# Stacks of k and q made while PSUM is emptied, f32 scores for four pairs, and the lower gate on GpSimd, in a new order of work

## The chip, the cores and the metric

One kernel runs on one core of a Trainium2 chip. The core has TensorE (PE; its weight loads are shown apart as PEld), VectorE (DVE), ScalarE (ACT), GpSimd (POOL) and SyncE (SP), each with its own queue of instructions that it takes in order; the engines wait for each other through semaphores. All DMAs of this kernel are issued by SyncE. The metric is the time of one execution on the device in microseconds, from first to last; lower is better.

## The reference

Attention over 4 batches of 8 heads, sequence 1152, head size 64, in which two neighbouring queries are averaged, followed by a two-layer network with a gate:

```
q_pool = q.reshape(B, H, S // 2, 2, D).mean(axis=3)        # 576 queries per head
scores = scale * q_pool @ k.T                              # 576 x 1152 per head
attn   = exp(scores - max); attn = attn / (sum + 1e-9)
x      = (attn @ v) as 2304 tokens of 512
h      = x @ w_in                                          # 512 -> 2048
g      = h * clip(h + 3, 0, 6) / 6
out    = g @ w_out                                         # 2048 -> 512
```

All inputs and the output are f32.

## The kernel before

**Attention.** Two heads of one batch make a pair; there are 16 pairs g. A pair has two halves h of 288 queries, and a half has two heads j; a unit u = (g, h, j) is one head's 288 queries against its 1152 keys, in 9 tiles t of 128 keys. Scores lie with keys on the partitions and queries in the columns. TensorE multiplies at f32r, one pass over 288 columns. To keep f32's precision, k and q are split into an upper part rounded to f32r (`kh`, `qh`) and the rest (`kl`, `ql`). The 128 partitions of a product hold 64 dimensions of the upper k and under them the same 64 of the lower k; q's upper part stands there twice, so that a first product takes both parts of k times `qh`, and a second one takes them times `ql` (L377).

The way to these stacks: `turn_k` (L324) and `turn_q` (L348) transpose a pair's k and pooled q on TensorE into PSUM, with one head in partitions 0 to 63 and the other in 64 to 127. `split` copies the upper part out on ScalarE (L330) and subtracts it on VectorE (L333). Since the halves have to go to other partitions, `move_k` (L340) and `move_q` (L355) then copy them from SBUF to SBUF by DMA: 12 DMAs per pair for k, 16 for q.

A unit goes on: `keep` copies a score tile from PSUM to SBUF on ScalarE (`copy`, L303), `most` takes the running maximum over tiles on VectorE (L390; for the first 15 units two key tiles at a time, with one fold at L394), `fold`, `best` and `spread` (L400, L404, L410) turn it into one maximum per query and lay it over all partitions, `lessen` (L414, VectorE) subtracts it, `expo` (L418, ScalarE) takes the exponential, `total` (L428, GpSimd) adds up over the tiles in four adds, `values` (L435) multiplies by v in f32, the two heads in two column groups of the array. `sums` (L452), `recip`, `widen`, `quotient` (L471) and `divide` (L475) scale the result; `split_x` and `spill` store it as f32r upper and lower part. `sums` frees the two tiles that the adds of the next half take.

**Network.** w_in and w_out are split once into upper and lower part by bit operations (`convert`: ScalarE, GpSimd, VectorE, L512 to L536), stored to DRAM (`save_w`) and loaded again for every 256 columns of x. A layer step m is one block of 128 hidden units for 256 tokens: `layer` (L184, 12 products), `relu` (L189, ScalarE), `gate` (L193, VectorE), `upper` (L197, ScalarE), `lower` (L202, the gated value minus its upper part; VectorE or GpSimd), and later `project` (L217, 6 products). 96 such steps are planned beside attention; the last 768 tokens follow in a loop of their own, with `lower` on VectorE.

**Order.** Nearly the whole program is a list of steps with a place (priority), costs per engine, needs, rooms taken and rooms freed. `Order.run` simulates the engines with these costs and so writes down one order for each engine; a tile framework adds the semaphores. `lower` may go to VectorE or GpSimd; its place there is 9 later (`NGL`). PSUM is divided anew once, at the step `second`: before it, attention has wide score tiles; after it, three banks for scores and banks for the network.

Of the kernel before, what the change touches and what calls it, by code (L numbers as in the profile page):

```python
# [11 lines left out]
F32 = mybir.dt.float32  # L12
F32R = mybir.dt.float32r
# [24 lines left out]
class Order:  # L38
# [14 lines left out]
    def run(self):  # L53
# [20 lines left out]
        while len(out) < len(steps):  # L74
# [4 lines left out]
            for e in engines:  # L79
# [20 lines left out]
                for b in frees:  # L100
                    if isinstance(b, tuple):
                        halves[b] = max(halves.get(b, 0), t + end + self.WAKE)
                        half[b] = half.get(b, 0) + 1
                        if half[b] < 2:
                            continue
# [22 lines left out]
def pooled_attention_then_gated_mlp(ctx, tc, q, k, v, w_in, w_out, out):  # L128
# [128 lines left out]
    with ExitStack() as a:  # L257
# [68 lines left out]
        def split(eng, tag, key, shape):  # L326
            ps = tr_t[key]
            if eng == "ACT":
                st = tr_t["st", key] = [ld.tile(shape, F32R, tag=tag + x, name=tag + x, bufs=2 if tag == "k" else 1) for x in "hl"]
                nc.scalar.copy(out=st[0], in_=ps)  # L330
            else:
                h, low = tr_t["st", key]
                nc.vector.tensor_tensor(out=low, in0=tr_t.pop(key), in1=h.bitcast(F32), op=ALU.subtract)  # L333

        def move_k(eng, g, c):
            if c == 0:
                kT[g] = kq.tile([P, 2, KT, P], F32R, tag="kT", name="kT")
            for n, x in enumerate(tr_t.pop(("st", ("k", g, c)))):
                for j in range(2):
                    nc.sync.dma_start(  # L340
                        out=kT[g][n * D:(n + 1) * D, j, KC * c:KC * (c + 1), :].bitcast(F32), in_=x[j * D:(j + 1) * D].bitcast(F32)
                    )

        def turn_q(eng, g, h):
            ps = tr_t["q", g, h] = space(g, HQ)
            for t in range(TQ):
                src = qp_t[g][:, h * TQ + t, :, :].rearrange("p j d -> p (j d)")
                nc.tensor.transpose(ps[:, t * QP:(t + 1) * QP], src, ident[:QP, :QP])  # L348

        def move_q(eng, g, h):  # L350
            q_t[g, h] = [qq.tile([P, 2, HQ], F32R, tag=t, name=t) for t in ("qh", "ql")]
            for x, to in zip(tr_t.pop(("st", ("q", g, h))), q_t[g, h]):
                for n in range(2):
                    for j in range(2):
                        nc.sync.dma_start(  # L355
                            out=to[n * D:(n + 1) * D, j, :].bitcast(F32), in_=x[j * D:(j + 1) * D].bitcast(F32)
                        )

        def index(u):
            return 4 * u[0] + 2 * u[1] + u[2]  # L360
# [18 lines left out]
        def keep(eng, u, t, end):  # L379
            if t == 0:  # L380
# [427 lines left out]
```

## Time and profile before

| | |
|---|---|
| median of 3 runs | 1052.11 us (1051.94 to 1064.61) |
| the profiled execution | 1051.82 us, its span 1050.0 us |
| mean granted TensorE clock | 0.927 |
| PE busy | 914.0 us (87%) |
| DVE busy | 709.1 us (68%) |
| ACT busy | 572.5 us (55%) |
| POOL busy | 500.2 us (48%) |
| DMA moved | 241.80 MB |
| chain of waits | PE 51%, DMA 22%, DVE 10%, issue 7%, ACT 5%, SPq 3% |

The span is the time from the first to the last instruction. "Busy" joins overlapping instructions of one engine; matmuls are pipelined and their ends are modelled. The chain of waits is followed back from the last instruction, at each step to what released it. In rows of busy time by stretch the engines stand as PE, PEld, DVE, ACT, POOL, each with its busy time and the count of its instructions. The granted clock is 1.00 where TensorE's clock is at its upper level. The pairs' first score products start at 20.5 us (pair 0), 61.3, 107.7, 151.2 and 202.7 us (pair 4); the first layer step at 235.5 us, and the last loop at 918.8 us.

### The profile page before, as it was taken

The page shows a single profiled execution, that of the slowest core. Times are in us where ns is not written, and L with a number is a line of the kernel's source. Part 1 is how long each engine was busy: PE and PEld are TensorE (multiplying, and loading weights), DVE is VectorE, ACT ScalarE, POOL GpSimd, SP SyncE. Part 2 cuts the span into 40 slices and gives each one's busy share as a digit, 9 for nine tenths or more (in the row PEclk, how much of TensorE's full clock was granted, in tenths as well). Part 3 has the DMA queues.
Part 4 walks back from the last instruction along what each step waited for, and adds up shares of the span by engine and source line. Part 5 has one row for each costly group of instructions (what it writes and reads, how often), then busy time and mean ns, then how long its engine had stood idle before and what let it go on. Part 6 is the DMA issues. An engine that isn't in the chain of part 4 may idle for free.

```text
span 1050.0 us, 17201 instructions
## 1 busy us (share of the span) xinstructions
PE 914.0 (87%) x5808; PEld 738.0 (70%) x5808; DVE 709.1 (68%) x1246; ACT 572.5 (55%) x1205; POOL 500.2 (48%) x417
## 2 busy tenths in 40 slices
PE   2687887788699999899889998998879989899997
PEld 2565565557567767687778786787768768788886
DVE  1797979787988886777667687676777764222222
ACT  1665767576476665666646565555546643222222
POOL 1376868774577675465355555344545544000000
PEclk9678877669898989999999999999989989999999
DMA  8898969698879998999998988998968747844332
GB/s 180 215 249 224 248 195 254 189 256 260 249 246 251 276 240 241 246 278 260 257 273 251 251 263 237 292 268 281 279 186 266 244 151 264 299 133 134 126 121 80
DMA packets 149240, 241.80 MB, mean 230 GB/s; under 512 B 51616, under 2 KB 103840, under 8 KB 149152
## 3 DMA queue, kind: packets, MB, share of 16 engines
q1 hardware_dynamic: 149152, 240.71, 78.9%
q8 instruction: 46, 0.75, 0.3%
q14 instruction: 42, 0.34, 0.1%
HBM read 171.97 MB, written 30.93 MB: 193 GB/s over the span
## 4 chain that ended last, share of the span: by engine, by line
PE 51%; DMA 22%; DVE 10%; issue 7%; ACT 5%; SPq 3%; POOL 2%; DVEq 0%; ACTq 0%; POOLq 0%
PE ph L184 13%; PE pav L435 11%; PE po L217 10%; DMA w<-w_d 9%; PE pqk L377 8%; DMA w_d<-scratch 4%; PE pt L217 4%; DVE m L390 3%; DVE gl L202 2%; DMA kT<-kl 2%; ACT s L303 2%; POOL d L428 2%; DVE s L414 1%; PE psr L452 1%; DMA raw<-in_moe_w_in_dram 1%
## 5 line engine op out<-in xcount | busy, mean ns | idle before, releaser
L303 ACT COPY s<-pqk 128x288 f32<-128x288 f32 (+1 forms) x516 | 206.7, 429 | 129.2 <-PE pqk L377 93.1
L377 PE MATMUL pqk<-qh,kT 128*128 128x288 f32 x576 | 208.9, 372 | 56.4 <-DVE m L390 31.6
L414 DVE TENSOR_TENSOR s<-s,pst 128x864 f32<-128x864 f32 x192 | 200.2, 1045 | 43.3 <-PE pst L410 43.0
L390 DVE TENSOR_TENSOR m<-pqk,m 128x288 f32<-128x288 f32 (+1 forms) x388 | 184.0, 474 | 57.6 <-PE pqk L377 25.4
L428 POOL TENSOR_TENSOR d<-s 128x864 f32<-128x864 f32 x64 | 132.7, 2083 | 156.1 <-PE psr L452 122.0
L184 PE MATMUL ph<-mxmxh,w 128*128 128x256 f32 x896 | 184.0, 288 | 20.2 <-DMA w<-w_d 18.6
L418 ACT ACTIVATE s<-s 128x864 f32<-128x864 f32 x192 | 178.1, 930 | 28.6 <-DVE s L414 26.3
L377 PEld LDWEIGHTS pqk<-qh,kT 128*128 128x128 f32 x576 | 121.4, 211 | 93.0 <-DVE m L390 37.4
L377 PE MATMUL pqk<-ql,kT 128*128 128x288 f32 x576 | 179.1, 320 | 4.5 <-DMA ql<-ql 4.5
L184 PEld LDWEIGHTS ph<-mxmxh,w 128*128 128x128 f32 x896 | 148.6, 193 | 26.8 <-DMA w<-w_d 15.7
L435 PE MATMUL pav<-s,vr 128*64 128x288 f32 x1152 | 162.4, 429 | 1.9 <-DVE scratch L529 1.9
L217 PE MATMUL po<-w,gh 128*128 128x512 f32 x448 | 143.7, 403 | 0.0
L189 ACT ACTIVATE r<-ph,three 128x256 f32<-128x256 f32 (+1 forms) x128 | 64.3, 503 | 138.9 <-PE ph L184 138.3
L428 POOL TENSOR_TENSOR d<-d,s 128x864 f32<-128x864 f32 x64 | 132.5, 2080 | 0.9
L377 PEld LDWEIGHTS pqk<-ql,kT 128*128 128x128 f32 x576 | 123.5, 214 | 7.2 <-issue 5.2
L202 DVE TENSOR_TENSOR gl<-r,gh 128x256 fp32r<-128x256 f32 (+1 forms) x104 | 107.7, 1035 | 30.3 <-ACT gh L197 29.2
L193 DVE SCALAR_TENSOR_TENSOR r<-r,ph 128x256 f32<-128x256 f32 (+1 forms) x128 | 57.4, 449 | 103.9 <-ACT r L189 103.7
L184 PE MATMUL ph<-mxmxl,w 128*128 128x256 f32 x448 | 127.5, 285 | 0.0
L435 PEld LDWEIGHTS pav<-s,vr 128*64 128x64 f32 x1152 | 80.5, 143 | 61.7 <-issue 17.5
L428 POOL TENSOR_TENSOR d<-d 128x288 f32<-128x288 f32 x128 | 105.3, 826 | 2.0
L217 PE MATMUL po<-w,gl 128*128 128x512 f32 x224 | 92.5, 413 | 10.6 <-DVE gl L202 8.9
L217 PEld LDWEIGHTS po<-w,gh 128*128 128x128 f32 x448 | 87.1, 194 | 15.3
(63 smaller groups left out, 1141.3 us busy)
## 6 DMA issues: line engine op xcount, KB each, us to landing
w<-w_d SPq DMA_DIRECT2D x224, 512.0 KB, 6.1
w_d<-scratch SPq DMA_DIRECT2D x32, 512.0 KB, 4.9
kr<-in_k_dram SPq DMA_DIRECT2D x32, 288.0 KB, 5.7
qr<-in_q_dram SPq DMA_DIRECT2D x16, 576.0 KB, 6.8
vr<-in_v_dram SPq DMA_DIRECT2D x16, 576.0 KB, 6.2
kT<-kh SPq DMA_DIRECT2D x96, 96.0 KB, 5.5
kT<-kl SPq DMA_DIRECT2D x96, 96.0 KB, 4.6
qh<-qh SPq DMA_DIRECT2D x128, 72.0 KB, 5.3
```

Source lines behind the costliest of these rows:

```text
L184: nc.tensor.matmul(ps, w[:, wi, cs], x[:, c, :], start=(m == 0), stop=(m == 3 * NCC - 1))
L189: nc.scalar.activation(out=r6, in_=ps, func=AF.Relu, bias=three)
L193: nc.vector.scalar_tensor_tensor(out=out, in0=r6, scalar=6.0, in1=ps, op0=ALU.min, op1=ALU.mult)
L202: on.tensor_tensor(out=gl, in0=r6, in1=gh.bitcast(F32), op=ALU.subtract)
L217: nc.tensor.matmul(o, g[:, ts], w[:, wi, :], start=(f == 0 and n == 0), stop=(f == NFC - 1 and n == 2))
L303: nc.scalar.copy(out=out, in_=in_)
L377: nc.tensor.matmul(ps[:, t - t0, 0:HQ], kT[g][:, j, t, :], w[:, j, :], start=(m == 0), stop=(m == 1))
L390: nc.vector.tensor_tensor(out=m, in0=ps_t[u, t][1][:, 0:n, 0:HQ], in1=s_t[u][:, 0:n] if first else m, op=ALU.max)
L414: nc.vector.tensor_tensor(out=s, in0=s, in1=st_t[u].unsqueeze(1).to_broadcast([P, KC, HQ]), op=ALU.subtract)
L418: nc.scalar.activation(out=s, in_=s, func=AF.Exp, scale=SCALE)
L428: by[eng].tensor_tensor(out=out, in0=x, in1=y, op=ALU.add)
L435: nc.tensor.matmul(av_t[g, h][j * D:(j + 1) * D, :], vr_t[g][:, j, t, :], s_t[g, h, j][:, t, :], start=(t == 0), stop=(t == KT - 1),)
```

## The change

- **k and q in stacks without DMA** (from pair 4 on). ScalarE copies the upper part of each head from PSUM straight to its place in the stack, and VectorE writes PSUM minus that to the other 64 partitions: `keep_k`, twice per three key tiles where there was one instruction of full height. q is pooled with its columns doubled (`pool_q`, n = 2), so that a transpose per head gives the head in both halves of the partitions; `turn_q` and `keep_q` run once per head j. The 28 DMAs per pair are gone.
- **f32 scores for pairs 0 to 3** (`EARLY = 4`). k and q aren't split; they are copied once from PSUM, by ScalarE or VectorE. A score tile is two f32 products of 64 partitions each, one head in partitions 0 to 63, the other in 64 to 127 (two row groups of the array), into two PSUM banks; the copy and the maximum take both heads at once (576 columns). The fold of L394 is gone.
- **Score tiles for two heads**: `SBUFS` 3 tiles of twice the size, freed by three steps instead of two.
- **`lower` on GpSimd alone** in the planned part.
- **Order**: new constants, costs and places, so that every engine's order changes.

```diff
-SBUFS = 6
-FIRST, STEPS, LAG = 100, (7, 2.74), 4
-CONV, CSTEP = 10, 9.97
+SBUFS = 3
+FIRST, STEPS, LAG = 89.54, (6.48, 2.86), 5.79
+CONV, CSTEP = 10, 8.78
 NEAR = 5
-WIDE, FCV = 15, 7
-ADDS = (4, 4, 0)
+EARLY, FCV = 4, 9
+ADDS = (2, 4, 0)
 CUT = 200
-PER, AT, NGL = 25.1, (-4, 6, -1.45, 3, 4.77, 20.2, 16.9), 9
+PER, AT, NGL = 25.1, (-3.22, 5.68, -1.34, 3.06, 4.65, 20.32, 16.96), 11.97
 TAIL = 768
...
         def pool_q(eng, g, j):
             if j == 0:
-                qp_t[g] = ld.tile([QP, QT, 2, D], F32, tag="qp", name="qp", bufs=1)
+                n = 1 if g < EARLY else 2
+                qp_t[g] = ld.tile([QP, QT, n, 2, D], F32, tag="qp", name="qp", bufs=1)
             x = qr_t[g][:, j]
-            by[eng].tensor_tensor(out=qp_t[g][:, :, j, :], in0=x[:, :, 0, :], in1=x[:, :, 1, :], op=ALU.add)
+            if g < EARLY:
+                by[eng].tensor_tensor(out=qp_t[g][:, :, 0, j, :], in0=x[:, :, 0, :], in1=x[:, :, 1, :], op=ALU.add)
+            else:
+                x, y = [x[:, :, r:r + 1, :].to_broadcast([QP, QT, 2, D]) for r in range(2)]
+                by[eng].tensor_tensor(out=qp_t[g][:, :, j, :, :], in0=x, in1=y, op=ALU.add)
...
-        def split(eng, tag, key, shape):
-            ps = tr_t[key]
-            if eng == "ACT":
-                st = tr_t["st", key] = [ld.tile(shape, F32R, tag=tag + x, name=tag + x, bufs=2 if tag == "k" else 1) for x in "hl"]
-                nc.scalar.copy(out=st[0], in_=ps)
+        def keep_k(eng, g, c):
+            if g not in kT:
+                kT[g] = kq.tile([P, 2, KT, P], F32R, tag="kT", name="kT")
+                if g < EARLY:
+                    kT[g] = kT[g].bitcast(F32)[:, 0]
+            cs = slice(KC * c, KC * (c + 1))
+            ps = tr_t["k", g, c]
+            if g < EARLY:
+                copy(eng, kT[g][:, cs], ps)
+                return
+            for j in range(2):
+                top = slice(j * D, (j + 1) * D)
+                if eng == "ACT":
+                    nc.scalar.copy(out=kT[g][top, j, cs], in_=ps[top])
+                else:
+                    nc.vector.tensor_tensor(
+                        out=kT[g][D - j * D:P - j * D, j, cs], in0=ps[top], in1=kT[g][top, j, cs].bitcast(F32), op=ALU.subtract
+                    )
+
+        def turn_q(eng, g, h, j):
+            ps = tr_t["q", g, h, j] = space(g, HQ)
+            for t in range(TQ):
+                src = qp_t[g][:, h * TQ + t, j].rearrange("p n d -> p (n d)")
+                nc.tensor.transpose(ps[:, t * QP:(t + 1) * QP], src, ident[:QP, :QP])
+
+        def keep_q(eng, g, h, j):
+            ps = tr_t["q", g, h, j]
+            if (g, h) not in q_t:
+                q_t[g, h] = [qq.tile([P, 2, HQ], F32R, tag=t, name=t) for t in ("qh", "ql")[:1 if g < EARLY else 2]]
+            hi = q_t[g, h][0][:, j]
+            if g < EARLY:
+                copy(eng, hi.bitcast(F32), ps)
+            elif eng == "ACT":
+                nc.scalar.copy(out=hi, in_=ps)
             else:
-                h, low = tr_t["st", key]
-                nc.vector.tensor_tensor(out=low, in0=tr_t.pop(key), in1=h.bitcast(F32), op=ALU.subtract)
-
-        def move_k(eng, g, c):
...
-        def move_q(eng, g, h):
...
         def scores(eng, u, t):
             g, h, j = u
...
+            if g < EARLY:
+                ps = ps_t[u, t] = ps_w.tile([P, 2, DM], F32, tag="v", name="pqk", bufs=2)
+                for j in range(2):
+                    d = slice(j * D, (j + 1) * D)
+                    nc.tensor.matmul(ps[:, j, 0:HQ], kT[g][d, t, :], q_t[g, h][0][d, 0, :].bitcast(F32), start=True, stop=True)
+                return
+            ps = ps_t[u, t] = ps_m["s"].tile([P, DM], F32, tag="s", name="pqk")
             for m, w in enumerate(q_t[g, h]):
-                nc.tensor.matmul(ps[:, t - t0, 0:HQ], kT[g][:, j, t, :], w[:, j, :], start=(m == 0), stop=(m == 1))
...
+                nc.tensor.matmul(ps[:, 0:HQ], kT[g][:, j, t, :], w[:, j, :], start=(m == 0), stop=(m == 1))
+
+        def parts(u, t):
+
+            g, h, j = u
+            if g < EARLY:
+                return ps_t[u, t][:, :, 0:HQ], s_t[g, h][:, :, t], s_t[g, h][:, :, 0], m_t[g, h]
+            return ps_t[u, t][:, 0:HQ], s_t[g, h][:, j, t], s_t[g, h][:, j, 0], m_t[g, h][:, j]
+
+        def keep(eng, u, t):
+            if t == 0 and u[2] == 0:
+                s_t[u[:2]] = sp.tile([P, 2, KT, HQ], F32, tag="s", name="s")
+                m_t[u[:2]] = sm.tile([P, 2, HQ], F32, tag="m", name="m", bufs=2)
+            ps, s, _, _ = parts(u, t)
+            copy(eng, s, ps)
+
+        def most(eng, u, t):
+            ps, _, s0, m = parts(u, t)
+            nc.vector.tensor_tensor(out=m, in0=ps, in1=s0 if t == 1 else m, op=ALU.max)
 
...
-            add(("gl", m), z, {"DVE": (520, 610), "POOL": (740, 760, NGL)}, partial(do_lower, m=m), [("gh", m)], (), ("r6",))
+            add(("gl", m), z, {"POOL": (700, 740)} if NGL else {"DVE": (520, 610), "POOL": (700, 740, -9)}, partial(do_lower, m=m), [("gh", m)], (), ("r6",))
```

What this does to the order is shown at two places. The first is the start of the program. TensorE's first instructions, before (`pt` is the PSUM tile of the transposes, `pqk` that of the scores):

```order
L324 MATMUL pt_128<-ident_58,kr_123 128x128 x3
L324 MATMUL pt_140<-ident_58,kr_123 128x128 x3
L324 MATMUL pt_154<-ident_58,kr_123 128x128 x3
L348 MATMUL pt_171<-ident_58,qp_138 128x96 x3
L348 MATMUL pt_179<-ident_58,qp_138 128x96 x3
L377 MATMUL pqk_207<-qh_183,kT_144 128x288
L377 MATMUL pqk_207<-ql_184,kT_144 128x288
```

The change (L329, L354 and L374 are its `turn_k`, `turn_q` and `scores`):

```order
L329 MATMUL pt_128<-ident_58,kr_123 128x128 x3
L329 MATMUL pt_136<-ident_58,kr_123 128x128 x3
L329 MATMUL pt_144<-ident_58,kr_123 128x128 x3
L354 MATMUL pt_152<-ident_58,qp_140 128x96 x3
L374 MATMUL pqk_160<-qh_158,kT_134 128x288 x2
L374 MATMUL pqk_163<-qh_158,kT_134 128x288 x2
L354 MATMUL pt_169<-ident_58,qp_140 128x96 x3
L374 MATMUL pqk_173<-qh_158,kT_134 128x288 x2
L329 MATMUL pt_182<-ident_58,kr_149 128x128 x3
```

The first score products stand behind three transposes of q instead of six, and no `ql` is among them. SyncE's queue of the start, before:

```order
L287 DMA kr_123<-in_k_dram 128x9x64 x2
L292 DMA qr_126<-in_q_dram 96x2x768
L297 DMA vr_132<-in_v_dram 128x2x576
L340 DMA kT_144<-kh_134 64x384 x2
L340 DMA kT_144<-kl_135 64x384 x2
L292 DMA qr_158<-in_q_dram 96x2x768
L287 DMA kr_160<-in_k_dram 128x9x64 x2
L340 DMA kT_144<-kh_150 64x384 x2
L340 DMA kT_144<-kl_151 64x384 x2
L355 DMA qh_183<-qh_175 64x288 x4
L355 DMA ql_184<-ql_176 64x288 x4
L340 DMA kT_144<-kh_163 64x384 x2
```

The change:

```order
L287 DMA kr_123<-in_k_dram 128x9x64 x2
L292 DMA qr_126<-in_q_dram 96x2x768
L297 DMA vr_132<-in_v_dram 128x2x576
L287 DMA kr_149<-in_k_dram 128x9x64 x2
L292 DMA qr_156<-in_q_dram 96x2x768
L297 DMA vr_179<-in_v_dram 128x2x576
L499 DMA raw_121<-in_moe_w_in_dram 128x4x256
L504 DMA raw_121<-in_moe_w_out_dram 128x1024
L287 DMA kr_214<-in_k_dram 128x9x64 x2
L292 DMA qr_225<-in_q_dram 96x2x768
```

The moves of k and q (L340, L355) are gone; the raw weights stand right behind the second pair's loads.

The second place is VectorE around layer step 70, before. L193 is `gate` (it writes `r6`), L202 `lower`, L390 a maximum of scores, L414 the subtraction of the maximum:

```order
L475 TENSOR_TENSOR x_8642<-psr_8648,x_8642 128x288
L193 SCALAR_TENSOR_TENSOR r6_8689<-r6_8689,ph_8659 128x256
L390 TENSOR_TENSOR m_8619<-pqk_8691,m_8619 128x288
L414 TENSOR_TENSOR s_8417<-s_8417,pst_8578 128x864
L202 TENSOR_TENSOR gl_8738<-r6_8689,gh_8712 128x256
L390 TENSOR_TENSOR m_8619<-pqk_8714,m_8619 128x288
L390 TENSOR_TENSOR m_8619<-pqk_8717,m_8619 128x288
L390 TENSOR_TENSOR m_8619<-pqk_8746,m_8619 128x288
L193 SCALAR_TENSOR_TENSOR r6_8752<-r6_8752,ph_8723 128x256
```

VectorE around the same step in the change (L396 and L416 are its maximum and subtraction, L366 the lower part of q, L406 `best`); step 70's gate is the first row:

```order
L193 SCALAR_TENSOR_TENSOR r6_7733<-r6_7733,ph_7695 128x256
L477 TENSOR_TENSOR x_7550<-psr_7676,x_7550 128x288
L406 TENSOR_REDUCE mq_7756<-pst_7740 96x3
L366 TENSOR_TENSOR ql_7781<-pt_7752,qh_7780 128x288
L366 TENSOR_TENSOR ql_7781<-pt_7762,qh_7780 128x288
L416 TENSOR_TENSOR s_7602<-s_7602,pst_7740 128x864
L396 TENSOR_TENSOR m_7603<-pqk_7791,s_7602 128x288
L193 SCALAR_TENSOR_TENSOR r6_7794<-r6_7794,ph_7766 128x256
L396 TENSOR_TENSOR m_7603<-pqk_7798,m_7603 128x288
L416 TENSOR_TENSOR s_7602<-s_7602,pst_7740 128x864
```

GpSimd there, where L430 is `total` and L485 `split_x`; the lower gate of step 70 reads `r6_7733`:

```order
L430 TENSOR_TENSOR d_7708<-s_7285 128x864
L430 TENSOR_TENSOR d_7730<-s_7285 128x864
L430 TENSOR_TENSOR d_7708<-d_7708,s_7285 128x864
L202 TENSOR_TENSOR gl_7789<-r6_7733,gh_7746 128x256
L430 TENSOR_TENSOR d_7708<-d_7708 128x288
L430 TENSOR_TENSOR d_7730<-d_7730,s_7285 128x864
L430 TENSOR_TENSOR d_7708<-d_7708 128x288
L485 TENSOR_TENSOR xl_7760<-x_7550,xh_7759 128x288
L430 TENSOR_TENSOR d_7730<-d_7730 128x288
L202 TENSOR_TENSOR gl_7871<-r6_7794,gh_7839 128x256
```

The lower gate has gone from VectorE's row to GpSimd's, behind three adds and before a fourth, and `ql` is made once per head.

## Rows read from the trace of the kernel before

**Rows 1.** Busy time by stretch: us, busy and count by engine, clock, DMA share, GB/s
```profile
20.50:202.70 182.20, 139.44 (x787) 101.24 (x787) 149.43 (x234) 117.57 (x205) 123.28 (x105) 0.78 0.81 222
412.60:805.00 392.40, 356.90 (x2528) 301.05 (x2526) 285.56 (x520) 234.37 (x535) 192.22 (x151) 0.98 0.90 258
918.80:1050.00 131.20, 125.46 (x630) 106.75 (x630) 35.57 (x63) 34.31 (x62) 0.00 (x0) 0.99 0.37 119
```

**Rows 2.** Groups of L202 (busy, mean ns): 203 to 918.8 us, then from 920 us
```profile
L202 DVE TENSOR_TENSOR gl<-r,gh 128x256 fp32r<-128x256 f32 x74 | 90.6, 1225 | 13.5 <-ACT gh L197 12.6
L202 POOL TENSOR_TENSOR gl<-r,gh 128x256 fp32r<-128x256 f32 x24 | 17.7, 739 | 101.4 <-ACT gh L197 92.6 <-issue 8.8
...
L202 DVE TENSOR_TENSOR gl<-r,gh 128x256 fp32r<-128x256 f32 x14 | 6.0, 426 | 6.6 <-ACT gh L197 6.6
```

**Rows 3.** Timeline: start us, us, engine, line, work [idle before, releaser]
```profile
272.74 4.02 POOL L428 TENSOR_TENSOR d<-s 128x864 f32<-128x864 f32 x2
273.73 7.97 DVE L202 TENSOR_TENSOR gl<-r,gh 128x256 fp32r<-128x256 f32 x1
276.72 3.96 POOL L428 TENSOR_TENSOR d<-d,s 128x864 f32<-128x864 f32 x2
281.76 0.79 PE L217 MATMUL po<-w,gl 128*128 128x512 f32 x1 [6.93 <-DVE gl L202]
...
745.39 0.53 PE L400 MATMUL pst<-ident,m 128*96 128x128 f32 x3 [3.19 <-DVE m L390]
```

**Rows 4.** Busy time in 25 us around the stop at 857 us
```profile
850.00:875.00 25.00, 19.87 (x133) 16.15 (x133) 16.01 (x21) 9.71 (x21) 11.98 (x9) 0.86 0.49 160
```

**Rows 5.** Timeline of the start, all engines
```profile
7.64 0.56 DVE L333 TENSOR_TENSOR kl<-pt,kh 128x384 fp32r<-128x384 f32 x1 [6.05 <-ACT kh L330]
...
10.32 0.90 PE L324 MATMUL pt<-ident,kr 128*128 128x128 f32 x3 [1.16 <-DVE kl L333]
...
17.19 2.48 SPq L355 DMA_DIRECT2D qh<-qh  x4
...
20.54 0.61 PE L377 MATMUL pqk<-qh,kT 128*128 128x288 f32 x1 [5.67 <-DMA qh<-qh]
```

**Rows 6.** Chain by line, 20.5 to 202.7 and 202.7 to 412.6 us; VectorE groups, 20.5 to 202.7
```profile
by line: issue 10.1%; DMA w_d<-scratch 9.8%; PE pav L435 9.1%; PE pqk L377 9.0%; DMA raw<-in_moe_w_out_dram 6.0%; DVE m L390 4.7%; DMA qh<-qh 4.5%; POOL d L428 4.0%; DMA vr<-in_v_dram 3.5%; SPq L355 3.5%; DMA qr<-in_q_dram 3.4%; DMA raw<-in
...
by line: DMA w_d<-scratch 12.8%; PE pav L435 11.4%; PE pqk L377 9.9%; DMA w<-w_d 6.7%; issue 5.6%; PE ph L184 5.4%; DVE gl L202 5.2%; PE po L217 5.0%; DVE m L390 4.5%; DMA raw<-in_moe_w_in_dram 4.1%; ACT s L303 3.8%; DMA kT<-kl 3.7%; DMA kT
...
L390 DVE TENSOR_TENSOR m<-pqk,m 128x576 f32<-128x576 f32 x30 | 22.5, 748 | 3.7 <-ACT s L303 3.6
...
L394 DVE TENSOR_TENSOR m<-m 128x288 f32<-128x288 f32 x15 | 13.1, 875 | 0.5
...
L333 DVE TENSOR_TENSOR kl<-pt,kh 128x384 fp32r<-128x384 f32 x13 | 7.2, 551 | 1.5 <-ACT kh L330 1.1 <-DMA kT<-kl 0.4
```

**Rows 7.** TensorE's timeline around 337 us; one piece of the chain of waits
```profile
336.83 0.30 PE L377 MATMUL pqk<-ql,kT 128*128 128x288 f32 x1
336.96 0.41 PE L348 MATMUL pt<-ident,qp 96*128 96x96 f32 x3
337.31 1.68 PE L435 MATMUL pav<-s,vr 128*64 128x288 f32 x12
338.91 0.53 PE L400 MATMUL pst<-ident,m 128*96 128x128 f32 x3
...
455.22 4.52 PE pav L435 x36
```

**Rows 8.** Waits: who waited for whom, us in total, times, longest
```profile
POOL d L428 <- PE psr L452: 122.0, 21, 13.3
...
PE ph L184 <- DMA w<-w_d: 18.6, 12, 3.1
```

**Rows 9.** DMA issues: count, KB each, median us to landing
```profile
kT<-kh SPq DMA_DIRECT2D x96, 96.0 KB, 5.5
...
qh<-qh SPq DMA_DIRECT2D x128, 72.0 KB, 5.3
```

More of the change, by code (lines that the diff above doesn't have):

```diff
@@ L103, in run @@
                         half[b] = half.get(b, 0) + 1
[L104 removed]
+                        if half[b] < 3:
                             continue
@@ L335, in move_k @@
-        def move_k(eng, g, c):
[L336 to L348, printed above, removed]
@@ L350, in move_q @@
-        def move_q(eng, g, h):
[L351 to L360, printed above, removed]
@@ L379, in keep @@
-        def keep(eng, u, t, end):
-            if t == 0:
-                s_t[u] = sp.tile([P, KT, HQ], F32, tag="s", name="s")
-            copy(eng, s_t[u][:, t:end], ps_t[u, t][1][:, 0:end - t, 0:HQ])
-        def most(eng, u, t, end):
-            n = end - t
-            first = pieces(u)[1][0] == t
-            if first:
-                m_t[u] = sm.tile([P, 2, HQ], F32, tag="m", name="m", bufs=2)
-            m = m_t[u][:, 0:n]
-            nc.vector.tensor_tensor(
-                out=m, in0=ps_t[u, t][1][:, 0:n, 0:HQ], in1=s_t[u][:, 0:n] if first else m, op=ALU.max
-            )
-            if end == KT and index(u) < WIDE:
-                nc.vector.tensor_tensor(out=m_t[u][:, 0], in0=m_t[u][:, 0], in1=m_t[u][:, 1], op=ALU.max)
+            if g < EARLY:
[4 more added lines that the diff above has]
+                return
@@ L627, in pooled_attention_then_gated_mlp @@
                     u = (g, h, j)
-                    before = (g, h, 0) if j else (g, h - 1, 1) if h else (g - 1, NH - 1, 1) if g else None
                     z0 = PER * g + UNIT * (2 * h + j)
-                    wide = index(u) < WIDE
-                    tag = "v" if wide else "s"
-                    ends = dict(pieces(u))
-                    for t in range(KT):
-                        end = t == KT - 1
-                        z = z0 + UNIT / KT * t
-                        add(("mm", u, t), z, {"PE": (268, 480)}, partial(scores, u=u, t=t),
-                            ([("mm", u, t - 1)] if t else [("mm", before, KT - 1)] if before else [])
-                            + ([("mq", g, h)] if not t else []) + [("mk", g, t // KC)]
-                            + ([("second",)] if index(u) == WIDE and not t else []),
-                            (tag,) if t in ends else (), (("q",) * j + ("kT",) * (h == NH - 1 and j)) if end else ())
@@ L641, in pooled_attention_then_gated_mlp @@
-                    for n, (t, e) in enumerate(pieces(u)):
-                        z = z0 + UNIT / KT * (e - 1)
-                        size = 50 + 245 * (e - t)
-                        add(("cp", u, n), z, {"ACT": (size, size + 80)}, partial(keep, u=u, t=t, end=e),
-                            [("mm", u, e - 1)] + ([("cp", u, n - 1)] if n else []), () if n else ("S",), ((tag, u, n),) if n else (tag,))
-                        if n:
-                            size = 68 + 300 * (e - t) + (380 if wide and e == KT else 0)
-                            add(("mx", u, n), z + .1, {"DVE": (size, size + 80)}, partial(most, u=u, t=t, end=e),
-                                [("mm", u, e - 1), ("mx", u, n - 1) if n > 1 else ("cp", u, 0)], ("m",) if n == 1 else (), ((tag, u, n),))
```

116 lines of the change are left out of this document (61 added, 55 removed).

## The prediction

> **What bounds the kernel now.** I read five views in this order. First the busy times by stretch [rows 1]: from 412.6 to 805.0 us, the long part in which attention and the network run side by side, TensorE is busy 356.90 of 392.40 us (91%) at a mean granted clock of 0.98, nearly always 2.4 GHz; only its own work and its stops count there. From 918.8 us on, the last 768 columns alone, it is busy 125.46 of 131.20 us, and the change leaves that code as it is. From 20.5 to 202.7 us it is different: TensorE 139.44 of 182.20 us at a clock of 0.78 (a mixture of 1.2 and 2.4 GHz), VectorE 149.43; no engine is full, so queues and waits decide. Second, the chain of waits of that stretch [rows 6]: beside TensorE's products it holds the stores of the weights' conversion, DMA qh<-qh with 4.5% and SyncE's own queue at L355 with 3.5%. Third, the groups of line L202 (`lower`) [rows 2]: the same subtraction of 128x256 takes VectorE 1225 ns on average before the last stretch (74 of them, 90.6 us) and 426 ns in it, where GpSimd is idle. Fourth, a timeline shows why [rows 3]: the one that starts at 273.73 us lasts 7.97 us, as long as GpSimd works through its adds without a pause, from 272.74 us on; TensorE stands still for 6.93 us until it ends. The waits and the DMA issues come last.
>
> **The change, part by part.** The profiled execution took 1051.82 us (span 1050.0 and 1.8 around it), 0.3 under the median of 1052.11; the sum is made against it.
>
> *The lower gate leaves VectorE.* In the new order all 96 of the planned ones are on GpSimd; VectorE has them in the last stretch alone. The five longest on VectorE made TensorE stand between 6.93 and 3.19 us each [rows 3], 24.1 together. In the 25 us stretches in which these five fall the clock is 0.86 to 0.93, the last as shown [rows 4], where 0.98 is the mean around them [rows 1]; 25 us times what each lacks to 1.00 is 13.5 us, and I count 10 of it, since TensorE had nothing to compute in some of that time. Lower end 24; upper end all that VectorE loses, 74 x (1.225 - 0.426) = 59 us. I take **-34**, near the lower end, which TensorE's own rows show. GpSimd pays 739 ns each [rows 2] for 72 more, 53 us on an engine that is busy 192.22 of 392.40 us [rows 1]; nothing, as long as TensorE has other work between a layer's step and its projection (rival two is the case in which it has not).
> The Trainium skill speaks against this part: "GPSIMD Engine Reference", Engine selection, sends elementwise work on a tile to VectorE, GpSimd being about twice as slow with two inputs. Alone the rows agree (739 against 426 ns); beside GpSimd's adds they do not (1225). By the rule this term would be nothing, and the sum 1022.
>
> *The start.* The first score product begins at 20.54 us, behind SyncE's issues of the moves that stack k and q (four of qh in 2.48 us, 0.6 each) and behind their landing [rows 5]. Now it needs three rounds of k's transposes and copies and one of q's. The third round of k begins at 10.32 us; the two subtractions of 0.56 us ahead of it are gone, so it begins near 9.2; three hand-overs of about 0.9 us each (transposes and copy) end near 12. **-8**, between 7 and 11.
>
> *The first four pairs.* VectorE loses the fold of two maxima (13.1 us) and the subtractions for k (7.2 us, and some 4 for q, of which pair 4 needs about half again), and its maxima become 64 of 748 ns (47.9 us) for 30 of these, 15 more of that size and 15 of half of it (43.8) [rows 6]: about 15 us less of 149. SyncE loses 28 issues per pair at 0.6 us, 17 us per pair, on the queue on which raw weights and conversion stores stand too; in the chain these moves held 4.5% + 3.5% of 182.2, 14.6 us. If another queue steps into the gap, the gain is 0; if both count in full, 27. **-14**, by VectorE's rows, the busiest engine there.
> The scores themselves: for a tile of 128 keys and both heads, four products at 0.13 us (336.83 to 336.96, [rows 7]) become two f32 products in different row groups. No such pair is in the trace. The nearest row is `values` [rows 7], f32 too, two heads in two column groups: 36 instructions, which are 18 products, in 4.52 us, 0.50 us for each two heads: 72 x (0.50 - 0.52), or -1. If two do not run together it is 1.00: 72 x 0.48 = +35 at full clock, +44 at 0.78. I take **+1**, near the nearest row.
>
> *Pairs 4 to 15.* q is transposed once per head with its columns doubled: 24 more groups of three, 0.35 us from the group at 336.96 to the next instruction [rows 7]; **+8**, all on TensorE. The emptying of PSUM goes in halves: per pair three more k subtractions of at most 0.55 us [rows 6] and two more of q, 2.6 us on VectorE, about as much on ScalarE, 31 us over 12 pairs. VectorE is 73% busy from 412.6 to 805 us [rows 1] and has just lost 90, ScalarE 60%: nothing; were that cover gone, it would be the 31. GpSimd's pooling of q writes twice as much, under 30 us in the idle half of GpSimd. The score tiles are held for two heads at a time, three of twice the size for six, and come free with the later head; no row of the waits shows anyone waiting for one.
> The moves of k and q are 2 x 96 x 96 KB and 2 x 128 x 72 KB [rows 9], 38 of the page's 241.8 MB. TensorE waited 18.6 us for w<-w_d [rows 8]; with a sixth of the traffic gone I take half, **-9**, between 0 and 18.6.
> From 202.7 to 412.6 us the chain holds 12.8% of conversion stores (27 us) and 3.7% of kT<-kl (8 us) [rows 6]. The new order has 24 layer steps ahead of pair 8's first score product, the old one 17, so work stands ready for the gaps. **-8**, the stacking alone; between 0 and 27.
>
> Sum: -34 - 8 - 14 + 1 + 8 - 9 - 8 = -64, **988 us**.
>
> **Rivals.** *One: the row groups cost more than they save.* Two f32 products of 64 rows run one after the other. Against it: the column groups do run together [rows 7]. For it: no row shows row groups. 988 + 44 - 1 = 1031. Chance 0.12.
> "TensorEngine Tiling (Array Packing)" of the Trainium skill, Key Properties, says that a change of tiling mode drains the engine. The twelve `values` instructions at 337.31 hold 1.60 us up to the next group, 0.09 more than a third of 4.52; with that bound for each of 144 changes it is 13 us, 1001 instead of 988, inside the range.
>
> *Two, slower than before: the lower gate waits on GpSimd.* GpSimd works in order; the first add of a half waits for the sums of the half before, 122.0 us in 21 waits, 5.8 each [rows 8]. A lower gate behind such an add stands still, and TensorE, in order too, at its projection. 24 halves from pair 4 on, 5.8 us each: +139, 1127 us. It decides where TensorE's work between a layer's step and its projection is shorter than the gate's other parts (about 1.3 us), two adds of some 2 us [rows 3] and 0.74 for itself: 6 us, or 12 with the wait. Counting the steps in the order at such durations as 0.27 us for two score products and 4.52 for `values` [rows 7], an estimate, the new order has 11 us there on average, the old 6.5. At 2.7 us per half the gain is gone, at 3.5 it is slower by 2%. Against it: no row of the waits has TensorE waiting for one of the 24 that GpSimd does now. Chance 0.08.
>
> *Three: the room is not used.* Outside the five long stops TensorE's next wait, for a weight, a copy or a sum, ends at the same time. Then 24 + 8 - 12 = 20 is left, 1032. Chance 0.12.
>
> *Four: more than counted.* All 59 us of VectorE and all of the 27 in the first four pairs come through: 988 - 25 - 13 = 950, say 955. Chance 0.13.
>
> That the moves or the VectorE gates stay after all is ruled out by the order.
>
> **The numbers.** The forecast has 0.55, with its own range from 970 to 1015. The range for 8 in 10 takes in rivals one and three and most of four: **955 to 1035**. Faster by over 2% (under 1031; 2% is about what a measurement of this kernel can tell from no change): 0.55 + 0.13 + half of one + a third of three = 0.78. Within 2%: the rest of one and three and 0.03 of two, 0.17. Slower: 0.05.
>
> **What would show it.** First score product near 12 us; no VectorE instruction over 1.1 us before the last stretch; no TensorE stop over 3 us behind a maximum; the first score product of pair 4 before 190 us (it is at 202.7, the end of a stretch of rows 1); two row-group products in 0.5 us; a last stretch of 131 us. I am wrong if the waits name the lower gate on GpSimd for more than 30 us of TensorE's time, if two row-group products take 1 us, or if the first four pairs take 180 us again.

## The result, and the profile after

The changed kernel takes 959.53 us (median of 4 runs, 956.26 to 964.33) where the kernel before took 1058.36 on the same chip (4 runs): a ratio of 0.907, 95% interval 0.898 to 0.916. The profiled execution took 957.85 us (span 956.1) where that of before took 1051.82: 94 us less, where I had forecast 64.

Busy time by stretch, of the kernel after. The five rows run from the first score product to that of pair 4, to that of pair 8, to that of pair 15, to the start of the last stretch, and to the end; columns as in [rows 1].
```profile
13.30:189.10 175.80, 146.78 (x795) 76.45 (x796) 141.79 (x216) 113.26 (x187) 131.41 (x116) 0.76 0.64 195
189.10:389.50 200.40, 187.00 (x1289) 146.90 (x1288) 167.20 (x328) 146.72 (x323) 150.25 (x131) 0.97 0.77 239
389.50:736.00 346.50, 346.01 (x2561) 296.25 (x2560) 253.20 (x506) 244.08 (x560) 235.12 (x201) 1.00 0.77 239
736.00:824.70 88.70, 86.57 (x605) 72.84 (x604) 43.76 (x89) 46.52 (x102) 47.17 (x43) 1.00 0.76 239
824.70:956.10 131.40, 124.72 (x627) 105.78 (x625) 34.82 (x62) 33.57 (x61) 0.00 (x0) 0.99 0.38 122
```
From 389.5 to 736.0 us TensorE pauses for 0.5 us in all, at 2.4 GHz throughout; in the part of before that answers to it, it was busy 91% at 0.98 [rows 1]. The first stretch is still at a clock of 0.76. Added up by stretch: start -7.2 (20.5 to 13.3), first four pairs -6.4 (182.2 to 175.8), from pair 4 to the last stretch -80.5 (716.1 to 635.6), last stretch +0.2. The 80.5 is the surprise; for it I had -43. It is read from one row of each kernel: TensorE alone, from pair 4 to the last stretch, first before, then after.
```profile
202.70:918.80 716.10, 644.98 (x4377) 0.95 0.86 254
```
```profile
189.10:824.70 635.60, 619.58 (x4451) 0.99 0.77 239
```
Its pauses fall from 71.1 to 16.0 us (length less busy), 55 of the 80; the other 25 are busy time at a better clock, with more instructions.

The lower gate of the kernel after: all planned ones on GpSimd, VectorE from 817.3 us on alone, where the loop of the last 768 tokens begins; answers to [rows 2].
```profile
L202 POOL TENSOR_TENSOR gl<-r,gh 128x256 fp32r<-128x256 f32 x96 | 70.3, 733 | 117.5 <-ACT gh L197 112.3 <-PE psr L454 4.9 <-PE po L217 0.2
...
L202 DVE TENSOR_TENSOR gl<-r,gh 128x256 fp32r<-128x256 f32 x16 | 6.8, 425 | 7.5 <-ACT gh L197 7.5
```
Its longest waits of TensorE:
```profile
PE pqk L374 <- DVE m L396: 18.7, 21, 2.5
PE pt L329 <- DMA kr<-in_k_dram: 7.7, 1, 7.7
PE psr L473 <- ACT rw L303: 6.9, 6, 3.3
```
Neither gl nor w<-w_d is among them: gl on GpSimd holds TensorE 0.3 us in all, w<-w_d 0.6 (18.6 in [rows 8]). So rival two is out.

What the waits hid, the chain of waits shows. In the long stretch of before (412.6 to 805 us), for which the prediction did not read it, it has a line that holds 20.0% of 392.4 us, 78 us:
```profile
by line: DMA w<-w_d 20.0%; PE pav L435 13.5%; PE po L217 11.3%; PE ph L184 10.5%; PE pqk L377 9.3%; issue 7.4%; DVE m L390 3.9%; DMA kT<-kl 3.0%; DVE gl L202 2.5%; PE psr L452 1.7%; POOL d L428 1.5%; DVE s L414 1.4%; PE pst L400 1.3%; DMA k
```
The 78 us are not what removing the loads would win: TensorE pauses 35.5 us in that stretch, 14.1 of them until a load of w lands, and the kernel after takes 45.9 us less there. In the same view of the kernel after, 389.5 to 736 us, no load stands in the part that is printed:
```profile
by line: PE ph L184 22.7%; PE po L217 22.0%; PE pqk L378 20.5%; PE pav L437 18.3%; PE psr L454 3.8%; PE pst L402 2.6%; PE pst L412 2.2%; PE pt L354 2.0%; PE pt L329 1.9%; PE psr L473 0.9%; DVE kT L346 0.9%; issue 0.7%; DVE m L396 0.5%; DVE 
```

Two row-group products of the kernel after, on TensorE's timeline at 2.4 GHz (x4 is one tile of both heads, x8 two):
```profile
27.03 1.24 PE L374 MATMUL pqk<-qh,kT 64*128 64x288 f32 x8
...
29.73 0.76 PE L374 MATMUL pqk<-qh,kT 64*128 64x288 f32 x4 [1.07 <-DVE m L396]
```
The second tile adds 0.48 us to the first, where rival one had 1.00 for a tile: rival one is out.

### The profile page after: what moved, and what is told of

Same layout as the page of the kernel before. It is cut to its first block, busy times and chain, and to the rows that moved or that the text cites. A ratio compares the mean times of both kernels' runs of the same rounds, so it can differ in the third digit from the quotient of the medians.

```text
span 956.1 us, 16751 instructions
## 1 busy us (share of the span) xinstructions
PE 894.5 (94%) x5880; PEld 700.2 (73%) x5880; DVE 642.0 (67%) x1204; ACT 587.3 (61%) x1237; POOL 564.7 (59%) x496
## 4 chain that ended last, share of the span: by engine, by line
PE 72%; DVE 8%; DMA 8%; ACT 4%; issue 4%; POOL 2%; SPq 1%; DVEq 0%; POOLq 0%; ACTq 0%
PE ph L184 18%; PE pav L437 14%; PE po L217 13%; PE pqk L378 11%; PE pt L217 5%; DMA w_d<-scratch 3%; DVE m L396 3%; PE pqk L374 3%; PE pst L402 2%; PE psr L454 2%; DMA raw<-in_moe_w_in_dram 2%; PE pst L412 2%; PE pt L329 1%; DVE s L416 1%; ACT s L420 1%
## 5 line engine op out<-in xcount | busy, mean ns | idle before, releaser
L396 DVE TENSOR_TENSOR m<-pqk,m 128x288 f32<-128x288 f32 (+1 forms) x392 | 193.6, 494 | 68.7 <-ACT s L303 61.2
L416 DVE TENSOR_TENSOR s<-s,pst 128x864 f32<-128x864 f32 x192 | 200.4, 1046 | 22.5 <-PE pst L412 22.0
L184 PE MATMUL ph<-mxmxh,w 128*128 128x256 f32 x896 | 180.8, 285 | 0.8 <-DVE r L193 0.8
L430 POOL TENSOR_TENSOR d<-s 128x864 f32<-128x864 f32 x64 | 131.4, 2058 | 52.1 <-PE psr L454 34.4
L378 PE MATMUL pqk<-qh,kT 128*128 128x288 f32 x432 | 140.4, 337 | 9.1 <-DVE m L396 5.2
L184 PEld LDWEIGHTS ph<-mxmxh,w 128*128 128x128 f32 x896 | 146.5, 190 | 3.3 <-DVE r L193 1.2
L202 POOL TENSOR_TENSOR gl<-r,gh 128x256 fp32r<-128x256 f32 x96 | 70.3, 733 | 117.5 <-ACT gh L197 112.3
L217 PE MATMUL po<-w,gh 128*128 128x512 f32 x448 | 139.6, 393 | 0.0
L430 POOL TENSOR_TENSOR d<-d,s 128x864 f32<-128x864 f32 x64 | 130.3, 2037 | 1.8 <-PE psr L473 1.0
L184 PE MATMUL ph<-mxmxl,w 128*128 128x256 f32 x448 | 126.5, 282 | 0.4 <-DMA mxmxl<-xl_d 0.4
L193 DVE SCALAR_TENSOR_TENSOR r<-r,ph 128x256 f32<-128x256 f32 (+1 forms) x128 | 57.4, 449 | 100.3 <-ACT r L189 100.0
L378 PE MATMUL pqk<-ql,kT 128*128 128x288 f32 x432 | 123.7, 298 | 0.0
L378 PEld LDWEIGHTS pqk<-qh,kT 128*128 128x128 f32 x432 | 82.5, 191 | 29.7 <-DVE m L396 13.6
L430 POOL TENSOR_TENSOR d<-d 128x288 f32<-128x288 f32 x128 | 101.9, 801 | 0.6
L217 PEld LDWEIGHTS po<-w,gh 128*128 128x128 f32 x448 | 84.3, 188 | 14.3
L184 PEld LDWEIGHTS ph<-mxmxl,w 128*128 128x128 f32 x448 | 85.1, 190 | 1.6 <-DMA mxmxl<-xl_d 0.7
```

What stands on the lines that cost most here:

```text
L184: nc.tensor.matmul(ps, w[:, wi, cs], x[:, c, :], start=(m == 0), stop=(m == 3 * NCC - 1))
L193: nc.vector.scalar_tensor_tensor(out=out, in0=r6, scalar=6.0, in1=ps, op0=ALU.min, op1=ALU.mult)
L202: on.tensor_tensor(out=gl, in0=r6, in1=gh.bitcast(F32), op=ALU.subtract)
L217: nc.tensor.matmul(o, g[:, ts], w[:, wi, :], start=(f == 0 and n == 0), stop=(f == NFC - 1 and n == 2))
L378: nc.tensor.matmul(ps[:, 0:HQ], kT[g][:, j, t, :], w[:, j, :], start=(m == 0), stop=(m == 1))
L396: nc.vector.tensor_tensor(out=m, in0=ps, in1=s0 if t == 1 else m, op=ALU.max)
```

## The experiments

Twelve kernels ran, each with three further rounds beside the kernel before; ratios are to before in the same job, 1% being 10.5 us. The change has three parts: the lower gate on GpSimd (G), the planner's numbers (N), the stacks without moves with the f32 pairs (S; the planner's new costs, `SBUFS`, `FCV` and the place of `second` go with it, and no kernel takes S apart). Six kernels hold combinations of them:

| parts in the kernel | median us | ratio, 95% interval | us against before |
|---|---|---|---|
| G (e1) | 1043.07 | 0.989, 0.974 to 1.005 | -11 |
| G, N (e10) | 1049.47 | 0.987, 0.979 to 0.995 | -14 |
| S (e9) | 1001.84 | 0.945, 0.938 to 0.951 | -58 |
| S, G (e4) | 989.95 | 0.940, 0.927 to 0.952 | -64 |
| S, N (e2) | 987.58 | 0.936, 0.919 to 0.953 | -67 |
| S, G, N (the change) | 959.53 | 0.907, 0.898 to 0.916 | -98 |

The last column is 1052 times what the ratio lacks to 1. The intervals reach 7 to 18 us to either side, and that of e1 takes in 1. Not all kernels ran in the same job; the change shares none with them, so its distance to another row carries both intervals.

**e1: the gate alone, in the kernel before.**
```diff
-{"DVE": (520, 610), "POOL": (740, 760, NGL)}
+{"POOL": (740, 760)}
```


> The kernel before with one edit: its planner may put the lower gate on GpSimd alone; stacks, moves and every other number of the order stay. Theory (VectorE held by GpSimd is the largest term, and all 59 us of it come back, more than the 34 I had taken): 995 to 1005 us where the kernel before takes 1058, and no VectorE instruction over 1.1 us ahead of the last stretch. Rival one (only TensorE's five long stops count): 1020 to 1030. Rival two (with the old distance of 4 between a layer's step and its projection, the gate is late on GpSimd): 1050 or more, and the waits name gl for over 20 us of TensorE.

Less than the theory or rival one had, and not told from nothing; TensorE waits 0.4 us for gl on GpSimd in all, so it isn't rival two. No VectorE gate is left ahead of the last stretch, though the sign failed: four folds of maxima (L394, two inputs in SBUF like the gate) still take 1.2 to 5.7 us in the first four pairs. From 406.6 to 800.6 us the kernel takes 394.0 us, where before took 392.4, and the chain now gives 23.4% to the loads of weights:
```profile
by line: DMA w<-w_d 23.4%; PE ph L184 15.4%; PE po L217 13.8%; PE pav L435 12.6%; PE pqk L377 11.6%; DMA kT<-kl 5.7%; PE psr L452 2.4%; SPq L340 2.0%; PE pst L400 1.6%; issue 1.6%; PE pst L410 1.2%; SPq L489 0.9%; PE pt L324 0.9%; DVE m L39
```
That fits rival three's mechanism: where VectorE would let TensorE go, a load comes late.

**e2: the gate undone in the changed kernel** (the lines of e1 the other way round, with 9 for NGL).


> The changed kernel with the lower gate planned for VectorE or GpSimd again, at the costs of the kernel before. Theory (59 us): 1010 to 1025 where the changed kernel takes 960; VectorE instructions of 2 to 8 us come back. Rival one (the long stops alone): 985 to 995. Rival (once the stacks are made at the emptying and the order is new, TensorE has other work and the gate is worth nothing): 955 to 970.

0.936 against 0.907: 31 us (28 by the medians), the first rival's size. VectorE takes 81 of them again, at 1002 ns where one alone takes 425 (excess 47 us); about two thirds come through:
```profile
L202 DVE TENSOR_TENSOR gl<-r,gh 128x256 fp32r<-128x256 f32 x81 | 81.2, 1002 | 16.8 <-ACT gh L197 16.2
```
The rule of the Trainium skill that I weighed in the prediction ("GPSIMD Engine Reference", Engine selection) would have the gate on VectorE; here that costs those 31 us. The same page's Specifications say that GpSimd shares its SBUF interfaces with VectorE, with contention where a VectorE instruction has two SBUF inputs; these rows agree and give the size.

**e4: the old numbers in the changed kernel.**
```diff
-FIRST, STEPS, LAG = 89.54, (6.48, 2.86), 5.79
-CONV, CSTEP = 10, 8.78
+FIRST, STEPS, LAG = 100, (7, 2.74), 4
+CONV, CSTEP = 10, 9.97
...
-PER, AT, NGL = 25.1, (-3.22, 5.68, -1.34, 3.06, 4.65, 20.32, 16.96), 11.97
+PER, AT, NGL = 25.1, (-4, 6, -1.45, 3, 4.77, 20.2, 16.9), 9
```


> The changed kernel with the planner's numbers of the kernel before (first layer step at 100, steps 7 and 2.74, lag 4, conversion every 9.97, the old offsets); code, costs and engines of the change stay. Theory (the numbers are worth about 20 of the 30 us that I did not count, by a fuller TensorE): 975 to 990 us. Rival (the numbers only follow the new costs and are worth nothing): 955 to 968. Third (with a lag of 4 the projections wait for GpSimd's gate): over 1000, and the waits name gl.

(`ADDS`, cut here, is set back too; its first number is used for no pair.) 0.940 against 0.907: 34 us, the upper end of the theory. gl on GpSimd holds TensorE's products for 1.1 us in all, so the third case is out. Counted on L184, 51 of the 128 layer steps stand behind pair 15's first product, 47 with the new numbers.

**e9 and e10: the stacks alone, and all but the stacks** (e4 with the edit of e2; e1 with the new numbers in place of the old).


> The changed kernel with both other parts undone: the planner's numbers and the choice of engine for the lower gate as before; only the stacks without moves, and the f32 pairs, are left. The kernel before takes 1058, the changed one 960; undone one at a time, the gate costs 28 and the numbers 30. Theory (the parts hold each other back: one alone gives less than it costs when it is undone last, and the stacks are the largest): 1005 to 1025. Rival (gate and numbers gain the same 30 by their own): 1015 to 1020 would need 58 in sum; over 1035 if the stacks alone give little, as the gate alone did.

> The kernel before with the lower gate on GpSimd alone and the planner's numbers of the change; the moves of k and q stay. Theory (SyncE's queue with its 28 moves per pair holds the layers' weights and the conversion, so neither a free VectorE nor an earlier layer step is of use): 1030 to 1055 where before takes 1058, the gate alone 1043. Rival (gate and numbers give their 28 and 30 wherever they stand): 995 to 1010.

The stacks alone give 58, a little more than expected, and in the chain of e9 from 414.0 to 770.8 us w<-w_d is not among the lines of 1.8% and more. All but the stacks give 14: with the moves, gate and numbers are nearly worthless, and in the chain of e10 from 431.5 to 837 us the loads stand second.
```profile
by line: PE ph L184 18.7%; DMA w<-w_d 18.4%; PE po L217 15.6%; PE pqk L377 11.4%; PE pav L435 9.7%; DMA kT<-kh 2.9%; PE psr L452 2.3%; SPq L355 2.3%; issue 2.0%; DVE m L390 1.8%; PE pst L400 1.8%; DMA qh<-qh 1.7%; DMA kT<-kl 1.5%; PE pst L4
```
On top of the stacks gate and numbers give 40 together, though only 6 and 9 one by one (differences that the intervals do not resolve).

The traces show where the numbers act (those of e9 and e10 are of their longest execution). From pair 15's first score product to the end, the kernels with the new numbers take 219 to 223 us, with the stacks or without (e10, e2, the change), those with the old ones 236 to 245 (e1, e9, e4, before): the four layer steps that no longer stand there have gone ahead. From pair 8's first score product to that of pair 15, the new numbers make it longer where the moves are left (405.5 us in e10, 394.0 in e1) or the gate is on VectorE (366.3 in e2, 356.8 in e9); with both gone they don't (346.5 in the change, 351.0 in e4), and TensorE is full.

**e3, e5, e6: what a move costs.** Moves that nobody waits for, put back into the changed kernel; the order on the four other engines stays.
```diff
+        def again(eng, n):
+            for _ in range(n):
+                i = parts_done[0] = (parts_done[0] + 1) % 8
+                a, b = i % 2 * D, (1 - i % 2) * D
+                nc.sync.dma_start(out=dy[i // 2][a:a + D], in_=dz[b:b + D])
...
+                add(("mk", g, c), z + 3 + c, {"SP": (1, 1, 0)}, partial(again, n=4), [("kl" if late else "kh", g, c)])
...
+                add(("mq", g, h), z + 1, {"SP": (1, 1, 0)}, partial(again, n=8), [("ql", g, h, 1) if late else ("qh", g, h, 0)])
```
(e5: 64x8 of a tile with room for all; e6: one issue for the 4 or the 8.)


> The changed kernel with 28 transfers per pair from SBUF to SBUF put back on SyncE's queue (64x288 from a constant tile to tiles that nobody reads, where the moves of k and q stood), so the traffic and SyncE's issues return and no product waits for them; the order on the four other engines is the same. Theory one (traffic and the queue cost what I took, 9 us in pairs 4 to 15 and about half of 14 in the first four pairs): +10 to +20 us, and TensorE waits for w<-w_d again. Theory two (it was the landing of the stacks that cost, not traffic or issues): within 4 us of the changed kernel.

> The changed kernel with the 28 issues per pair on SyncE's queue as in e3_moves_back, but each moves only 64x8 values (2 KB instead of 74 KB), to places that never wait for an earlier move. e3_moves_back took 1029 us, 70 more than the changed kernel; theory one (the price is the queue: 28 issues in order, with the waits ahead of them): 1010 to 1030. Theory two (the price is the traffic on the DMA engines): 960 to 975. Between them both count.

> The changed kernel with the whole 2.06 MB per pair of e3_moves_back, in 5 issues instead of 28 (three of 128x2x288, two of 128x4x288). Theory one (the queue's issues): 960 to 975. Theory two (the traffic): 1010 to 1030.

e3 takes 1029.41 us (0.976, 0.963 to 0.989), e5 996.89 (0.941, 0.937 to 0.944), e6 974.98 (0.920, 0.917 to 0.923): +72, +36 and +14 us by the ratios. e3 is far beyond what either theory had; e5 falls between its two, e6 ends at the top of theory one's. The queue's issues are the larger part, the traffic a smaller one, and e3, which has both, costs more than their sum. By stretch, from the traces:

| us | first four pairs | pairs 4 to 7 | pairs 8 to 14 |
|---|---|---|---|
| after | 175.8 | 200.4 | 346.5 |
| e3: 28 issues, 2.06 MB per pair | 202.9 | 223.5 | 369.4 |
| e5: 28 issues, 57 KB | 202.5 | 212.7 | 351.4 |
| e6: 5 issues, 2.06 MB | 186.8 | 205.8 | 346.7 |

In the first pairs it is the queue. Timeline of e5, SyncE's queue and the engines that stand behind it (L327 is the moves, L510 the load of raw weights, L525 the conversion's first step; the kernel after issues that load at 14.48 us):
```profile
21.58 4.95 SPq L327 DMA_DIRECT2D dy<-dz  x8
26.57 0.59 SPq L510 DMA_DIRECT2D raw<-in_moe_w_in_dram  x1
30.34 0.66 ACT L525 ACTIVATE scratch<-raw 128x512 f32<-128x512 f32 x1 [10.16 <-DMA raw<-in_moe_w_in_dram]
31.55 0.76 DVE L407 TENSOR_TENSOR m<-pqk,m 128x576 f32<-128x576 f32 x1 [10.58 <-ACT s L303]
32.36 2.59 PE L385 MATMUL pqk<-qh,kT 64*128 64x288 f32 x8 [7.38 <-DVE m L407]
```
Eight moves of 2 KB hold the queue 4.95 us, 0.62 each; the load behind these and twenty earlier ones starts 12.1 us later than in the kernel after, ScalarE stands 10.16 us for it with score copies queued behind that step, VectorE for the copies, TensorE for the maxima. In pairs 8 to 14, neither small moves nor few large ones cost more than 5 us, but 28 full ones cost 23, and w<-w_d is back in e3's chain with 9.8%. There SyncE's queue also stands still ahead of e3's moves until a load of weights has landed, though no move reads a weight (58.8 us in 51 waits; e5 has 22.5 in 30):
```profile
SPq L327 <- DMA w<-w_d: 58.8, 51, 3.0
```
e3's moves write eight places in turn and may wait for earlier moves too, e5's don't; so whether the excess of e3 over the sum comes of issues and traffic meeting or of these waits, no run separates. e6's queue stands 33.7 us for its own earlier moves, 27.5 of them in the first pairs, so its 14 us are not of the traffic alone either. In these three the planner did not know of the moves; e10, where it did and where S is missing whole, is 84 us behind the change (0.987 against 0.907).

"DMA: Bandwidth & Descriptors" of the Trainium skill, Issuing engines are not separate DMA queues, calls the sequencer's time to start a transfer usually small relative to the transfer. For 512 KB loads the rows agree (0.59 us for one, 4.7 to landing by the median in e5); for moves of 2 KB in a row on one queue they don't (4.95 us for eight, 3.3 to landing).

**e7, e8: products of constants into spare columns of the score tiles, first four pairs.**
```diff
+                for x in range(2):
+                    nc.tensor.matmul(ps[:, x % 2, HQ:HQ + 224], identr, fill, start=True, stop=True)
```


> The changed kernel with two products of constants (128x224, some 0.11 us each at full clock) behind the score products of each of the 72 tiles of the first four pairs, into columns of the same tile that nobody reads; they change no result. Theory (in these pairs the granted clock of 0.76 costs the time that I expected to gain, and TensorE's pauses behind maxima are what keeps it there): a clock over 0.85 there, the four pairs in 160 to 170 us instead of 175.8, 945 to 957 in all. Rival (VectorE and the conversion bound these pairs, and the clock only follows): 16 to 30 us of extra work, of which the pauses hide most: 958 to 970, and the clock where it was.

> As e7_fill_2 with five such products per tile (360 in all, some 40 us at full clock). Theory (the clock): over 0.95 in the first four pairs, 155 to 170 us for them, 940 to 955 in all. Rival (other engines bound them): TensorE becomes the bound at the clock it had, 190 us or more for them, 970 to 990.

974.19 us (0.919, 0.916 to 0.923) and 983.10 (0.928, 0.925 to 0.932). The first four pairs of e8:
```profile
11.50:211.00 199.50, 180.72 (x1155) 115.04 (x1156) 143.30 (x216) 114.56 (x187) 132.61 (x117) 0.91 0.55 172
```
The clock follows the work (0.84 in e7, 0.91 here), but the pairs take longer (188.1 and 199.5 us). e7 is slower than both cases had it; e8 is where its rival put it, though with the clock up, which the rival had not. The price of the half clock they do not give, since the score copies waited for the fills. These are ScalarE's waits in the first four pairs, of the kernel after and of e8, in which L380 is the fill:
```profile
ACT s L303 <- PE pqk L374: 32.9, 32, 4.5
...
ACT s L307 <- PE pqk L380: 67.9, 56, 4.4
```

**e11: a shorter conversion on VectorE.**
```diff
+            few = 64 if f < FCV else DM
...
-                    out=t, in0=size.bitcast(U32), scalar1=3, scalar2=0x3FFFFFF8,
+                    out=t[:, 0:few], in0=size[:, 0:few].bitcast(U32), scalar1=3, scalar2=0x3FFFFFF8,
```
(likewise the two steps behind it; the kernel leaves most of these weights unconverted)


> The changed kernel; the three steps of the weights' conversion on VectorE work on 64 of 512 columns for the nine blocks ahead of pair 4, so most columns of these weights are not converted. It takes about 19 x 3 x 0.57 = 32 us from VectorE's 141.8 in the first four pairs. Theory one (VectorE bounds these pairs, and the low clock only follows): they take 150 to 160 us instead of 175.8, the whole 935 to 945. Theory two (TensorE at half clock and the order of hand-overs bound them): 168 to 176, the whole 952 to 960.

953.04 us (0.897, 0.892 to 0.903). Theory two: VectorE loses 22.7 us in the first four pairs (32 were expected), and they get 5.4 shorter.
```profile
12.60:183.00 170.40, 144.34 (x796) 75.46 (x796) 119.10 (x216) 112.36 (x187) 130.82 (x116) 0.79 0.64 201
```

**e12: the weights' stores issued by GpSimd** (`nc.gpsimd.dma_start` in `save_w`).


> The changed kernel with the 32 stores of converted weights issued by GpSimd, which has just made them, instead of SyncE, which stands 48 us in 22 waits for them with other loads behind it; the order of the four engines' other work is the same. Theory (SyncE's queue is still short in the first pairs): 6 to 15 us less there, 945 to 954. Rival (after the moves went, the queue is no longer on the path, and each issue costs GpSimd about 1 us): 957 to 972.

969.36 us (0.912, 0.906 to 0.918): the rival's time, at 0.60 us for an issue on GpSimd where it had about 1. The first four pairs take 178.9 us instead of 175.8. Since the 32 issues also hold GpSimd for 19.2 us, e12 does not tell what they still cost on SyncE. No kernel here that does all the work beats the changed one.

## Why the prediction was right, and where not

- **Start, -8: right.** First product at 13.3 us, -7.2.
- **Row groups, +1: right.** 0.48 us for the pair of products of a further tile, where 0.50 was taken from `values` [rows 7].
- **The lower gate, -34: the size holds only when the moves are gone and the numbers are new.** 31 when undone last (e2), 11 alone (e1), 6 on the stacks with the old numbers (e4 against e9). I argued it from the kernel before, where TensorE's five stops were real, but late loads stood behind them (e1's chain). The 24 I gave as a lower end was no lower end. That 34 is close to the 40 of gate and numbers together is luck in part: the numbers had no term.
- **w loads, -9, and the stretch to 412.6, -8: the step that failed.** I priced the loads by TensorE's row of waits, 18.6 us [rows 8], and took from [rows 1] that "only its own work and its stops count there". The chain of that stretch has the loads at 20.0%, and in e9 it is 35.6 us shorter (356.8), with the gate still on VectorE. A late load also holds what stands in order behind it on other engines, and TensorE then waits under other names, for maxima or sums; e5's rows show this for the raw weights. All that I had on the stacks sums to -30 (-8 - 14 + 1 + 8 - 9 - 8); e9 gives 58 for it. I had also counted SyncE's issues only ahead of pair 4; e5 has them cost 12 in pairs 4 to 7 as well.
- **The order: no term of mine.** The numbers are worth 34 undone last (e4) and nothing to be seen with the moves there (e10 against e1). Why gate and numbers need each other on top of the stacks, 40 together, no run shows by itself. The traces fit this: the numbers move four layer steps ahead of pair 15, and the pairs before it take them in without growing only where neither late loads nor VectorE's gate hold TensorE. That the plan has longer between a layer's step and its projection, which a gate on GpSimd uses, is only argued too.
- **First four pairs, -14: -6.4.** I went by VectorE as the busiest engine. (In its sum of maxima, the "15 of half of it" are 22 of 0.45 us in the trace; 43.8 is right.) e11 shows that it isn't the bound: with 22.7 us less of it, 5.4 are won. TensorE is busy 146.78 of 175.80 us there at a clock of 0.76, a mixture of 1.2 and 2.4 GHz; the pauses behind maxima come on top, and what VectorE lost did not shorten TensorE's own work. What these pairs would take at 2.4 GHz stays open (e7 and e8 could not show it).
- **q twice, +8, and the extra emptying on ScalarE and VectorE, 0:** not tried apart. In pairs 8 to 14 TensorE pauses 0.5 us in all, so nothing there speaks against 0.
- **Rival four** had the size (955) for the wrong reasons: neither all of VectorE's 59 nor the 27 of the first pairs came through.

The signs held: no VectorE instruction over 1.06 us ahead of the last stretch, no stop of TensorE over 2.5 us behind a maximum, pair 4 at 189.1 us (just under the 190), a last stretch of 131.4. The forecast's own range, 970 to 1015, was missed. The 959.53 lies 5 us inside the wide one, and 0.907 of the 1052 that the sum started from would be 954, just outside. It came out that low because all of S was mis-sized by some 28 us; that the moves are the part of it that was mis-sized rests on e3, e5 and e6, not on a kernel that takes S apart.

## What to carry to other kernels

Ask the chain of waits for every stretch before a term is priced, above all for the one that looks full: a row of waits names only the last releaser, and here 18.6 us of waits went with 78 us of chain. Neither was the price, which only a kernel with the cause removed shows: that stretch became 35.6 us shorter with the stacks alone (e9). Count short transfers by their issues on the queue that they share and by what is loaded behind them, and not by their bytes alone. Where two limits lie on one path, the worth of removing one is read only with the other gone: the gate was worth 11 us before, an interval that takes in 0, and 31 after.

## What the runs showed of the hardware

- 448 moves of 2 KB cost 36 us, 2.06 MB per pair in few moves 14, 448 moves with these bytes 72, more than the sum; part of that may be moves that wait for earlier ones.
- Two f32 products with 64 rows each, in different row groups, take 0.48 us beyond the pair before them.
- A VectorE subtraction of 128x256 with two inputs in SBUF takes 425 ns alone and 1002 on average beside GpSimd's adds (e2), up to 7.97 us [rows 3].
- Products of constants in TensorE's pauses lift the granted clock (0.76 to 0.84 and 0.91) without a gain, since their time and the waits behind them cost more.
